# An attention and feed-forward block: a third staging buffer for the query and key products, the masking band in bf16, and weight preparation queued one microsecond behind its operands

## The chip, the core and the metric

The kernel runs on one core of one Trainium2 chip. The metric is the device time of one launch in microseconds. A core has five instruction queues that matter here: TensorE (PE, matrix products; its weight loads are shown as PEld), VectorE (DVE), ScalarE (ACT), GpSimdE (POOL) and SyncE (SP). SyncE only issues DMA transfers; ScalarE issues some as well, between its other instructions. Each queue runs in the order in which the program was written.

## The reference

One transformer block on 2048 rows of 640, with 32 heads of 20 and a window of 256 keys:

```
def _A_ref(x, wqkv, wo):
    qkv = (x @ wqkv).reshape(B, S, 3, H, Dh).transpose(2, 0, 3, 1, 4)
    q, k, v = qkv[0], qkv[1], qkv[2]
    scores = einsum("bhqd,bhkd->bhqk", q, k) * (Dh ** -0.5)
    mask = (idx[:, None] - idx[None, :] >= 0) & (idx[:, None] - idx[None, :] < W)
    scores = where(mask, scores, -1e9)
    o = einsum("bhqk,bhkd->bhqd", softmax(scores), v)
    return o.transpose(0, 2, 1, 3).reshape(B, S, D) @ wo

def _B_ref(x, w_gate, w_up, w_down):
    return (gelu(x @ w_gate) * (x @ w_up)) @ w_down

h  = x + _A_ref(layernorm(x), wqkv, wo)
h2 = h + _B_ref(layernorm(h), w_gate, w_up, w_down)     # F = 1536
```

Everything is float32.

## The kernel before

Float32 accuracy at half-precision speed comes from splitting. A matrix is written as a high half and a low half in float16 (names ending in `h` and `l`), and a product is made of three: high by high, low by high, high by low (`products`, L550). The first rows' value product is the exception: it runs on raw float32 weights held in `gu`, `h0h` and `h0l`. Where the planner finds room it runs a product as four products on quarters of the array side by side (`quarters`, L542).

The rows are cut in 16 blocks of 128 (`B[j]`) and 8 pairs of blocks (`c`). For each block the kernel loads the rows (`xt`), normalises them (`xp`), transposes the halves (`xh`, `xl`), and then a pair of blocks goes through the query and key products (`qk`, L736). `qk_out` (L761) evicts such a product from PSUM: ScalarE copies the high half into a staging tile `qks`, VectorE the low half, and ScalarE issues a DMA that writes both to a scratch tensor in DRAM, `qk<c><0 or 1>` (0 for queries, 1 for keys). `stack` (L783) reads it back with SyncE, six small copies for each stack, in the layout in which the score products need their operands (`qT`, `kT`). So `qk21` are the keys of pair 2, and the six copies `kT<-qk21` are one of its two stacks. The staging tile has two buffers, and `qk_out` starts only while fewer than two of the `qks` are unwritten: `pos["qk"]` counts those begun, `pos["qks"]` those whose write is issued.

For each block and each head, scores are computed twice. First come `maxima`: a product, on which `max_out` (L925) runs a VectorE operation that adds a mask and takes the row maximum. The mask is `band` (L614) for inner blocks: zero, with a large negative number above and below the allowed diagonals. Then comes the score product, transposed, with the maximum folded in as further rows; ScalarE takes the exponential into `pt`, GpSimdE clears what the window excludes, and TensorE multiplies by the values (`pv<-pt,v`). The result goes through the output projection `w3` into `h`, and the feed-forward part follows in three groups of 512 columns. Its last groups work on sums of halves (`ws`), made from the split weights after attention, when their buffers come free.

Weights are prepared beside attention. `load_slices` (L375) loads a 128-row slice (`wsl`) twice: once for VectorE to find the scale (`scale`, L389; its reduction reads the slice into `am`), and once for `split` (L435): ScalarE writes the high half (`gu<-wsl`), scales the slice in place (`wsl<-wsl`), and GpSimdE subtracts to get the low half. The output projection comes first (`wo`), then the first group's gate slices (from `in_wg_dram`) and up slices (from `in_wu_dram`).

What runs when is decided as the program is written, by a planner. `Clock` (L54) holds a modelled time for each engine, for each tile and for each DMA. Work is divided into lanes (generators), and a lane yields the engine that it wants and a function for the modelled time at which its operands are ready. The loop at the end steps a modelled time `now`; `Lane.start` (L1832) lets a lane queue its next instruction if its engine is free soon enough (`back`) and its operands are ready by `now + late`. `late` is 0.1 us, or minus `HELD` (1 us) for most of SyncE's transfers. So the instruction order on every queue is fixed by these numbers, and a small edit can move much. `split_lane` (L1679) and `scale_lane` (L1649) are the lanes of the weights. Until the first score is queued, the loop fills TensorE with products of the unit matrix (`pv<-ident16`, L1914) wherever nothing else is ready.

One property of the queues is seen in the instruction lists: SyncE's and ScalarE's DMAs take turns on eight landing semaphores. A DMA that gets a semaphore waits until the DMA that had it last has landed, also if that was issued by the other engine and has nothing to do with it.

All instructions are recorded by a helper, `Engine.call` (L199), so every row of the profile carries L199, and rows are told apart by the names of their tiles.

Of the kernel before, what the change touches and what calls it, by code (L numbers as in the profile page):

```python
# [11 lines left out]
F32 = mybir.dt.float32  # L12
F16 = mybir.dt.float16
BF16 = mybir.dt.bfloat16
# [8 lines left out]
P = 128  # L23
# [4 lines left out]
CW = 2 * P  # L28
# [21 lines left out]
def _pow2(e):  # L50
    return float(2.0 ** e)
# [202 lines left out]
def block_kernel(ctx: ExitStack, tc: tile.TileContext, x, wqkv, wo, wg, wu, wd, out):  # L254
    nc = Clock(tc.nc)
    const = ctx.enter_context(tc.tile_pool(name="const", bufs=1))
# [10 lines left out]
    opened, pos = Counter(), Counter()  # L267
# [14 lines left out]
    def done(name):  # L282
        opened[name] -= 1
# [23 lines left out]
    SWAY = 4  # L307
    BRIDGE = 0.2
    PATIENCE = 2.0

    def need(*reads, slots=(), when=None, eng="tensor"):

        def f():
            if when and not when() or any(opened[n] >= banks[n] for n in slots):
                return INF
            return max([nc.ready(reads, eng)]
                       + [nc.slot(psums[n], n, banks[n]) for n in slots])
        return f
# [4 lines left out]
    def on(eng, *reads, when=None, after=None):  # L323
        f = need(*reads, when=when, eng=eng)
        if after is not None:
            return (eng,), lambda: max(f(), nc.others(after, eng))
        return (eng,), f
# [14 lines left out]
    nc.vector.tensor_copy(ident16, ident)  # L342
    mhalf = const.tile([P, 1], F32, name="mhalf")
    nc.vector.memset(mhalf, -0.5)
    ones = const.tile([P, P], F32, name="ones")
    nc.vector.memset(ones, 1.0)


    NS = 16
# [110 lines left out]
    W = {}  # L460
# [89 lines left out]
    def products(n, term, ready=None, at_=None):  # L550


        ps = [at_[0]] if at_ else []
        col = at_[1] if at_ else 0

        def start(i):
            if ready and not ready(i) or not ps and opened["mm"] >= banks["mm"]:
                return INF
            t = nc.ready([x for ab in term(i) for x in ab], "tensor")
            return t if ps else max(t, nc.slot(psums["mm"], "mm", banks["mm"]))  # L560

        for i in range(n):
            yield ("tensor",), lambda i=i: start(i)
            if not ps:
                ps.append(bank("mm"))
            m = term(i)
            for k, (l, r) in enumerate(m):
                if k:
                    yield pe()
                o = ps[0][:, col:col + r.free_size()]  # L570
                quarters(o, l, r, start=(i == 0 and k == 0),
                         stop=(i == n - 1 and k == len(m) - 1))
                pos["dense"] += r.free_size() * 3 // len(m)
        return o
# [12 lines left out]
    def ff_scales_down(fg):  # L587
# [6 lines left out]
    wq = wqp.enter_context(tc.tile_pool(name="wq", bufs=1, side="right"))  # L594
    wp = attn.enter_context(tc.tile_pool(name="wp", bufs=1))
# [13 lines left out]
    HB = P // 2  # L609
# [1 line left out]
    nc.gpsimd.memset(mask, 0.0)  # L611
    nc.gpsimd.affine_select(mask[:, P:2 * P], mask[:, P:2 * P], pattern=[[-1, P]],
                            compare_op=ALU.is_ge, fill=NEG, base=0, channel_multiplier=1)
    band = wp.tile([P, 5 * HB], F32, name="band")  # L614
    nc.gpsimd.memset(band, 0.0)
    for a in range(2):
        first, last = band[HB * a:HB * a + HB, 0:HB], band[HB * a:HB * a + HB, 4 * HB:]
# [36 lines left out]
    qs = const.tile([P, 1], F32, name="qs")  # L654
# [81 lines left out]
    def qk(c, which):  # L736

        w = W["qk"[which]]
        first = c == which == 0
        if not first:  # L740
            xh, xl = C[c].x
            wh, wl = w.hl
        d = dram.tile([D, 2, CW], F16, name=f"qk{c}{which}")
        left = [3]
        for t0 in range(0, KC, 2):
            ts = range(t0, min(t0 + 2, KC))
            yield pe(slots=["mm"])
            ps = bank("mm")
            for i, t in enumerate(ts):
                fs = slice(t * P, (t + 1) * P)  # L750
                if first:
                    yield from products(KC, lambda k: [(w.raw[0, k][:, fs], x32[:, k, :])],
                                        at_=(ps, i * CW))
                    continue
                yield from products(KC, lambda k: parts((wh[:, k, fs], wl[:, k, fs]),
                                                        (xh[:, k, :], xl[:, k, :])),
                                    lambda k: k in w.have, (ps, i * CW))
            tasks.append(qk_out(c, which, ts, ps, d, left))
        C[c].used += 1

    def qk_out(c, which, ts, ps, d, left):  # L761

        o = ps[:, :len(ts) * CW].rearrange("p (t n) -> p t n", n=CW)
        up = qs if c == which == 0 else _pow2(QE)
        yield on("scalar", ps, when=lambda: pos["qk"] < pos["qks"] + 2 and (c or pos["qs"]))
        pos["qk"] += 1
        st = nc.tile(wq, [P, 2, 2, CW], F16, "qks", 2)
        hi, lo = (st[:, :len(ts), i, :] for i in range(2))
        nc.scalar.activation(hi, o, AF.Copy, scale=up)
        yield on("vector", hi, after=ps)  # L770
        nc.vector.scalar_tensor_tensor(lo, o, up, hi, op0=ALU.mult, op1=ALU.subtract)
        done("mm")
        both = st[:, :len(ts)].rearrange("p t m n -> p t (m n)")
        yield on("scalar", both)
        nc.scalar.dma_start(d[ts[0] * P:(ts[-1] + 1) * P].rearrange("(t p) m n -> p t (m n)", p=P),
                            both)
        pos["qks"] += 1
        left[0] -= 1
        if not left[0]:
            for blocks in [[2 * c, 2 * c + 1]] if c < 2 else [[2 * c], [2 * c + 1]]:  # L780
                side.append((LATE, stack(c, which, d, blocks)))

    def stack(c, which, d, blocks):  # L783
        last = blocks[-1]
        yield ("sync",), need(d, when=lambda: pos["big"] == 2 and (W["q"].ready if c < 2 else
                                                                B[last - 4].scored), eng="sync")
        if which == 0:
            for b in blocks:
                B[b].mx = at("mxs", [P, H], F32, 4)
        ring, n = ((qT, RQ), (kT, RK))[which]  # L790
        s = blocks[0] % n
        to = ring[:, :, s:s + len(blocks), :].rearrange("p i r n -> p i (r n)")
        cols = slice(blocks[0] % 2 * P, blocks[-1] % 2 * P + P)
        for par in range(2):
            for m, i in enumerate(((0, 0, 1), (0, 1, 0))[which]):
                rows = slice(64 * par + DH * m, 64 * par + DH * m + DH)
                if c > 1:
                    yield ("sync",), lambda: nc.moved["sync"] - PACE
                nc.sync.dma_start(to[rows], d.rearrange("(a d i) m n -> a m d i n", a=2,
                                                        d=DH)[par, i][:, :, cols])  # L800
        for b in blocks:
            B[b].stacked += 1
            if B[b].stacked == 2:
                for pr in range(0, H // 2, pairs(b)):
                    heapq.heappush(maxq, (b, pr))
# [327 lines left out]
    ffpools = [None, None]  # L1133
# [685 lines left out]
    class Lane:  # L1819
# [12 lines left out]
        def start(self, now):  # L1832

            if "tensor" in self.engs:
                if (self.gen.__name__ in ("normalise", "o_transpose") and nc.mode == "col"
                        and not B[-1].scored and self.need() <= nc.t["tensor"]):
                    self.since = min(self.since, nc.t["tensor"])
                    if nc.t["tensor"] < self.since + PATIENCE:
                        return False
                wait = BRIDGE if nc.kind == "col" and self is rows else 0.0  # L1840
                return (nc.t["tensor"] <= now + AHEAD
                        and self.need() <= max(now, nc.t["tensor"]) + wait)
            name = self.gen.__name__
            back = self.back
            if name in ("split_lane", "scale_lane"):
                back = PREP if not W["o", 0].ready else FFPREP
            elif name == "x_lane":
                back = EARLY if not B[XF].full else LATE
            elif name == "max_out" and not W["v"].ready:
                back = RAMPMAX  # L1850
            if isinstance(self.engs, Soon):
                back = max(back, OUT)
            if ffpools[1]:
                back = FFBACK.get(name, OUT)
            late = 0.1 if self.engs != ("sync",) or name in ("stack", "load_lane") else -HELD
            return (all(nc.t[e] <= now + back for e in self.engs if e != "sync")
                    and self.need() <= now + late)

# [109 lines left out]
```

## Time and profile before

| | |
|---|---|
| time, median of 3 runs | 1001.67 us (1001.38 to 1004.41) |
| the profiled execution: time, span | 1003.55 us, 1001.8 us |
| TensorE products, weight loads | 15101 each |
| VectorE, ScalarE, GpSimdE instructions | 2246, 859, 498 |
| DMA traffic | 112.97 MB, 113 GB/s on average |
| first score maximum on TensorE | 53.20 us |
| last exponentials and values of attention | about 562 us |
| lowest granted clock of the 40 slices | 0.8, in the slice from 150 us |

A page of the profile gives each engine's busy time and its share of the span, then the span in 40 slices with the busy tenths and the clock that TensorE was granted, then the chain of work that ended last, followed back from the last instruction. The trace behind the page is asked for stretches, timelines of an engine, single tiles and waits. In a row `out<-in` names the tile written and those read, with partitions and elements; `x4` means that many such instructions; the bracket gives the idle time of the engine ahead of the row and what ended it. Products are pipelined, so their lengths overlap, and what one costs is the distance of two starts.

### The profile page before, as it was taken

Reading aid. Unit: us, or ns where it says so; the run is one execution under the profiler, and the core shown is the slowest. Engines: PE = TensorE matmul, PEld = TensorE weight load, DVE = VectorE, ACT = ScalarE, POOL = GpSimd, SP = SyncE. Lnnn points to the kernel's source line nnn. Section 1 sums busy time; section 2 is a strip of 40 time slices with the busy share of each in tenths; the row PEclk is TensorE's granted clock in tenths of the full one; section 3 lists DMA queues with packets and bytes.
Section 4 is the critical chain, followed back from the end, with each engine's and each line's share of the span. In section 5 each row is a group of like instructions: output and inputs, shape, how many; then the busy total and the mean of one; then the engine's idle time right before and its main releaser. Section 6 shows DMA issues by size and latency. Waiting matters only on the chain.

```text
span 1001.8 us, 35343 instructions
## 1 busy us (share of the span) xinstructions
PE 979.5 (98%) x15101; PEld 747.0 (75%) x15101; DVE 788.6 (79%) x2246; ACT 486.4 (49%) x859; POOL 340.9 (34%) x498
## 2 busy tenths in 40 slices
PE   8998997999999999999999999999999999999998
PEld 8875775777787777777656754588788888888886
DVE  7878997887877876676688697897986877788784
ACT  5516564855555655555577634343223333443431
POOL 7003344544433433333345301253403222232320
PEclk9999998999999999999999999999999999999999
DMA  8657755652433523123315342234453442223211
GB/s 312 130 129 170 174 144 162 161 131 64 106 94 71 116 77 95 50 75 83 122 30 140 61 143 81 82 130 133 132 185 100 144 152 79 79 75 112 80 54 53
DMA packets 129613, 112.97 MB, mean 113 GB/s; under 512 B 85168, under 2 KB 103344, under 8 KB 129456
## 3 DMA queue, kind: packets, MB, share of 16 engines
q1 hardware_dynamic: 117360, 99.97, 35.6%
q10 hardware_dynamic: 12096, 10.75, 3.5%
q8 instruction: 118, 1.93, 0.8%
q14 instruction: 39, 0.32, 0.1%
HBM read 73.73 MB, written 28.84 MB: 102 GB/s over the span
## 4 chain that ended last, share of the span: by engine, by line
PE 77%; DVE 6%; DMA 2%; ACT 2%; issue 1%; POOL 1%; SPq 0%; ACTq 0%; DVEq 0%; POOLq 0%
PE mm L199 35%; PE rb L199 12%; PE ra L199 11%; PE pv L199 10%; PE tp L199 9%; DVE ts L199 1%; DVE am L199 1%; DVE gel L199 1%; DMA wst<-in_wu_dram 1%; DVE al L199 1%; DVE ws L199 0%; DVE ht L199 0%; DVE junk L199 0%; DMA wsl<-in_wg_dram 0%; DMA qk<-qks 0%
## 5 line engine op out<-in xcount | busy, mean ns | idle before, releaser
L199 POOL TENSOR_SCALAR_AFFINE_SELECT pt<-pt 128x512 f32<-128x512 f32 x352 | 174.8, 512 | 272.6 <-ACT pt L199 254.5
L199 DVE CUSTOM_DVE_ANT_0 junk<-ra,band 128x320 bf16<-128x320 f32 x230 | 112.5, 489 | 42.8 <-PE ra L199 37.7
L199 ACT ACTIVATE pt<-rb,esc 128x640 f32<-128x640 f32 (+2 forms) x131 | 99.7, 768 | 92.9 <-PE rb L199 77.2
L199 DVE CUSTOM_DVE_ANT_0 junk<-rb,band 128x320 bf16<-128x320 f32 x218 | 106.6, 489 | 34.6 <-PE rb L199 29.6
L199 ACT ACTIVATE pt<-ra,esc 128x640 f32<-128x640 f32 (+2 forms) x125 | 95.0, 767 | 73.1 <-PE ra L199 61.5
L199 PE MATMUL pv<-pt,v 128*21 128x128 f32 x2880 | 103.5, 276 | 0.8 <-ACT oT L199 0.6
L199 PEld LDWEIGHTS <-ah 128*128 128x128 f16 x648 | 63.4, 98 | 23.5 <-issue 1.2
L199 PEld LDWEIGHTS <-ws 128*128 128x128 f16 x720 | 70.4, 98 | 13.0 <-issue 3.0
L199 PEld LDWEIGHTS <-qT 60*64 60x64 f16 x1280 | 29.8, 104 | 65.7 <-issue 55.4
L199 PEld LDWEIGHTS pv<-pt,v 128*21 128x21 f32 x2880 | 69.3, 101 | 10.5 <-issue 1.0
L199 PEld LDWEIGHTS <-kT 62*64 62x64 f16 x2880 | 64.7, 107 | 10.3 <-issue 6.9
L199 PEld LDWEIGHTS <-gu 128*128 128x128 f16 (+1 forms) x709 | 51.9, 98 | 25.7
L199 DVE SCALAR_TENSOR_TENSOR ht<-mm,ffk,ht 128x320 f32<-128x320 f32 x86 | 46.9, 545 | 16.4 <-PE mm L199 15.2
L199 PE MATMUL mm<-xh,w1h 128*32 128x256 f16 (+1 forms) x356 | 56.6, 276 | 1.4 <-DVE qks L199 1.4
L199 PE MATMUL mm<-xl,w1h 128*32 128x256 f16 (+1 forms) x368 | 56.5, 276 | 0.0
L199 PE MATMUL mm<-xh,w1l 128*32 128x256 f16 (+1 forms) x362 | 56.5, 274 | 0.0
L199 ACT CAST ah<-gel 128x512 f16<-128x512 f32 x48 | 29.6, 617 | 53.3 <-DVE gel L199 51.8
L199 DVE TENSOR_TENSOR al<-gel,ah 128x512 f16<-128x512 f32 x48 | 42.9, 893 | 14.9 <-ACT ah L199 14.2
L199 ACT ACTIVATE gel<-gel,ffk 128x512 f32<-128x512 f32 x36 | 26.0, 722 | 54.5 <-DVE gel L199 54.4
L199 PE MATMUL mm<-w3h,ol 128*32 128x320 f16 (+1 forms) x322 | 49.6, 301 | 0.0
L199 PE MATMUL mm<-w3l,oh 128*32 128x320 f16 (+1 forms) x319 | 49.4, 301 | 0.0
L199 PE MATMUL mm<-w3h,oh 128*32 128x320 f16 (+1 forms) x310 | 49.4, 299 | 0.0
(354 smaller groups left out, 2670.0 us busy)
## 6 DMA issues: line engine op xcount, KB each, us to landing
ws<-wsums SPq DMA_DIRECT2D x24, 640.0 KB
qk<-qks ACTq DMA_DIRECT2D x32, 256.0 KB
wsums<-ws SPq DMA_DIRECT2D x12, 640.0 KB
qT<-qk SPq DMA_DIRECT2D x72, 80.0 KB
kT<-qk SPq DMA_DIRECT2D x72, 80.0 KB
ht<-in_x_dram SPq DMA_DIRECT2D x16, 320.0 KB
h_dram<-ht SPq DMA_DIRECT2D x16, 320.0 KB
ht<-h_dram SPq DMA_DIRECT2D x16, 320.0 KB
```

The source lines that it names most:

```text
L199: r = real(*args, **kw)
```

## The change

Four edits:

- The staging tile `qks` gets three buffers instead of two, and `qk_out` may start while fewer than three are unwritten. That takes 2048 bytes more of each partition.
- `band` is kept in bf16 instead of float32 (640 bytes a partition less). Its values are 0 and -1e30.
- `ones`, a float32 tile of 128 by 128 that nothing reads, is left out (512 bytes less).
- In `Lane.start`, once the output projection is ready and until the feed-forward buffers are open, work of `split_lane` and `scale_lane` is queued only if its operands have been ready for one modelled microsecond (`SETTLE`).

```diff
@@ -307,6 +307,7 @@
     BRIDGE = 0.2
     PATIENCE = 2.0
+    SETTLE = 1.0
@@ -342,8 +343,6 @@
-    ones = const.tile([P, P], F32, name="ones")
-    nc.vector.memset(ones, 1.0)
@@ -611,7 +610,7 @@
-    band = wp.tile([P, 5 * HB], F32, name="band")
+    band = wp.tile([P, 5 * HB], BF16, name="band")
@@ -762,9 +761,9 @@
-        yield on("scalar", ps, when=lambda: pos["qk"] < pos["qks"] + 2 and (c or pos["qs"]))
+        yield on("scalar", ps, when=lambda: pos["qk"] < pos["qks"] + 3 and (c or pos["qs"]))
         pos["qk"] += 1
-        st = nc.tile(wq, [P, 2, 2, CW], F16, "qks", 2)
+        st = nc.tile(wq, [P, 2, 2, CW], F16, "qks", 3)
@@ -1853,6 +1852,8 @@
             late = 0.1 if self.engs != ("sync",) or name in ("stack", "load_lane") else -HELD
+            if name in ("split_lane", "scale_lane") and W["o", 0].ready and not ffpools[0]:
+                late = -SETTLE
             return (all(nc.t[e] <= now + back for e in self.engs if e != "sync")
                     and self.need() <= now + late)
```

Since the planner's order follows from these numbers, the instructions move. TensorE has 14046 matrix instructions in the program instead of 13603; all of the difference comes from products that run as four quarters (829 instead of 651), and fillers are 144 instead of 235. The order of the last 2813 products is unchanged. Three places:

**TensorE before the first maxima.** Before, the raw value product (`mm<-gu`, `mm<-h0h,gu`, `mm<-h0l,gu`) alternates with small transposes, and where it stops waiting for room, the fillers begin (`pv<-ident`; a run of 86 of them follows).

```order
L199 MATMUL mm<-gu 128x320
L199 MATMUL ra<-ident,am_386 128x128
L199 MATMUL mm<-h0h,gu 128x320
L199 MATMUL rb<-ident,pt 128x128 x4
L199 MATMUL tp<-ident,pt 128x128
L199 MATMUL mm<-h0h,gu 128x320
L199 MATMUL mm<-h0l,gu 128x320 x2
L199 LDWEIGHTS ident_81
L199 MATMUL pv<-ident_81 128x128
```

Now, on the same queue and at the same place:

```order
L199 MATMUL mm<-gu 128x320
L199 MATMUL mm<-h0h,gu 128x320
L199 MATMUL tp<-ident,pt 128x128
L199 MATMUL mm<-h0h,gu 128x320
L199 MATMUL mm<-h0l,gu 128x320
L199 MATMUL rb<-ident,pt 128x128
L199 MATMUL mm<-h0l,gu 128x320
L199 MATMUL mm<-gu 128x320
L199 MATMUL mm<-h0h,gu 128x320 x2
L199 MATMUL mm<-h0l,gu 128x320 x2
L199 LDWEIGHTS w0h
```

The fillers at this place are gone, and the query products (`w0h`) follow at once. The value product of the second block pair moves behind the first maxima, and 184 products of 256 columns stand ahead of the first maximum instead of 97.

**SyncE around the last gate slices.** Before, the two last gate slices (`wsl<-in_wg_dram`) stand among the copies of the key stacks of pair 2 (`kT<-qk21`):

```order
L199 DMA xt_2815<-in_x_dram 128x640
L199 DMA kT_126<-qk21_2287 20x16x128 x2
L199 DMA ht_2949<-in_x_dram 128x640
L199 DMA kT_126<-qk21_2287 20x16x128 x5
L199 DMA wsl_3044<-in_wg_dram 128x512
L199 DMA kT_126<-qk21_2287 20x16x128
L199 DMA wsl_3088<-in_wg_dram 128x512
```

Now these stacks are through before, and the first up slices (`wsl<-in_wu_dram`) stand among the stacks of pair 3 (`qT<-qk30`, `kT<-qk31`):

```order
L199 DMA_TRANSPOSE xl_2951<-xp_3027 128x5x128
L199 DMA xt_3371<-in_x_dram 128x640
L199 DMA wsl_3673<-in_wg_dram 128x512
L199 DMA wsl_3716<-in_wg_dram 128x512
L199 DMA qT_125<-qk30_2568 20x16x128 x2
L199 DMA wsl_3770<-in_wu_dram 128x512
...
L199 DMA kT_124<-qk31_3164 20x16x128
L199 DMA wsl_3940<-in_wu_dram 128x512
L199 DMA kT_124<-qk31_3164 20x16x128 x3
L199 DMA wsl_4005<-in_wu_dram 128x512
L199 DMA wsl_4007<-in_wu_dram 128x512
```

The two gate slices moved out of the key stacks, and four up slices (numbers 3770, 3940, 4005 and 4007 here) moved in among the stacks of the next pair.

**ScalarE at the last gate splits.** Before, the split of a slice (`gu<-wsl`, `wsl<-wsl`) stands between the exponentials (`pt`) that follow the 40th, and the write of `qk30` (`DMA qk30<-qks`) directly ahead:

```order
L199 DMA qk30_2653<-qks_3048 128x512
L199 ACTIVATE pt_3100<-ra_3101,esc_130 128x2x320
L199 ACTIVATE gu_99<-wsl_2605,sw_88 128x512
L199 ACTIVATE wsl_2605<-wsl_2605,sw_88 128x512
L199 ACTIVATE pt_3100<-rb_3155,esc_130 128x2x320
L199 ACTIVATE gu_99<-wsl_3044,sw_88 128x512
L199 ACTIVATE wsl_3044<-wsl_3044,sw_88 128x512
```

Now, with the exponentials that follow the 48th:

```order
L199 ACTIVATE pt_3793<-ra_3794,esc_128 128x2x320
L199 DMA qk40_3644<-qks_3783 128x2x512
L199 ACTIVATE gu_97<-wsl_3673,sw_86 128x512
L199 ACTIVATE wsl_3673<-wsl_3673,sw_86 128x512
L199 ACTIVATE gu_97<-wsl_3716,sw_86 128x512
L199 ACTIVATE pt_3793<-rb_3844,esc_128 128x2x320
L199 ACTIVATE wsl_3716<-wsl_3716,sw_86 128x512
```

The splits moved eight exponentials further down, behind the first write of `qk40`; the splits of the up slices moved from the 54th to 59th exponential to the 69th to 74th.

## The prediction

> **What bounds the kernel now.** I read the page first: busy time of each engine, the granted clock, and the chain that ended last.
>
> ```profile
> PE 979.5 (98%) x15101; PEld 747.0 (75%) x15101; DVE 788.6 (79%) x2246; ACT 486.4 (49%) x859; POOL 340.9 (34%) x498
> PEclk9999998999999999999999999999999999999999
> PE 77%; DVE 6%; DMA 2%; ACT 2%; issue 1%; POOL 1%; SPq 0%; ACTq 0%; DVEq 0%; POOLq 0%
> PE mm L199 35%; PE rb L199 12%; PE ra L199 11%; PE pv L199 10%; PE tp L199 9%; DVE ts L199 1%; DVE am L199 1%; DVE gel L199 1%; DMA wst<-in_wu_dram 1%; DVE al L199 1%; DVE ws L199 0%; DVE ht L199 0%; DVE junk L199 0%; DMA wsl<-in_wg_dram 0%; DMA qk<-qks 0%
> ```
>
> TensorE is busy for 98% of the span and makes 77% of the chain. The change leaves its useful products as they are, so it can only win the time in which TensorE waits, runs fillers or has a lower clock. The clock row has one 8, in the slice from 150 to 175 us. The next view is therefore the table of busy time by stretches (span, then PE, PEld, DVE, ACT, POOL, granted clock, DMA share, GB/s).
>
> ```profile
> 24.00:76.00 52.00, 50.59 (x533) 40.23 (x533) 41.73 (x158) 19.68 (x40) 1.65 (x3) 1.00 0.63 128
> 92.00:100.00 8.00, 5.56 (x79) 3.25 (x81) 7.15 (x23) 5.34 (x9) 3.99 (x4) 0.83 0.72 201
> 158.00:163.20 5.20, 0.62 (x24) 0.38 (x13) 0.57 (x4) 2.20 (x4) 0.70 (x2) 0.89 0.69 171
> 163.20:170.00 6.80, 6.80 (x93) 4.54 (x93) 5.03 (x15) 2.36 (x5) 3.56 (x6) 0.58 0.62 193
> 200.00:450.00 250.00, 249.89 (x6263) 193.88 (x6255) 188.71 (x701) 142.00 (x220) 99.35 (x206) 1.00 0.35 88
> ```
>
> From 200 to 450 us TensorE loses 0.11 us of 250: nothing is to be had there. The holes are before. The largest is at 158 us, and the timelines of TensorE and of ScalarE say what it is (start, length, operation, and in brackets the idle time before it and what ended it).
>
> ```profile
> 158.11 0.35 PE L199 MATMUL mm<-w3h,ol 128*32 128x320 f16 x4
> 158.25 0.35 PE L199 MATMUL mm<-w3h,oh 128*32 128x320 f16 x4
> 163.18 0.48 PE L199 MATMUL ra<-kT,qT 60*64 60x320 f16 x4 [4.58 <-ACT pt L199]
> ```
>
> ```profile
> 155.24 0.77 ACT L199 ACTIVATE pt<-rb,esc 128x640 f32<-128x640 f32 x1
> 160.91 0.72 ACT L199 ACTIVATE gu<-wsl,sw 128x512 f16<-128x512 f32 x1 [4.90 <-DMA wsl<-in_wg_dram]
> 162.35 0.78 ACT L199 ACTIVATE pt<-ra,esc 128x640 f32<-128x640 f32 x1
> ```
>
> TensorE waits 4.58 us for a score exponential (`pt<-ra`), and that stands in ScalarE's queue behind a weight split (`gu<-wsl`) whose slice has not landed. Why the slice is late stands in SyncE's timeline, its waits between 130 and 200 us, and the chain of waits from 142 to 165 us.
>
> ```profile
> 148.81 7.64 SPq L199 DMA_DIRECT2D kT<-qk  x5
> 156.55 0.46 SPq L199 DMA_DIRECT2D wsl<-in_wg_dram  x1
> ```
>
> ```profile
> SPq L199 <- DMA qk<-qks: 13.1, 5, 3.8
> ```
>
> ```profile
> 142.98 3.65 DMA qk<-qks
> ...
> 156.55 4.33 DMA wsl<-in_wg_dram
> ```
>
> Five stack copies took 7.64 us of SyncE's queue. One copy alone takes about 0.75, so half of it is a wait, 3.8 us at the longest, for the landing of a `qk` write which ScalarE issued. SyncE's and ScalarE's transfers share a ring of landing semaphores, so a stack copy can wait for a write that it doesn't read. The slice is issued at 156.55 and lands 4.33 us later.
>
> **The change, part by part.** Sums are against the profiled execution, 1003.55 us (span 1001.8 and 1.75 around it). It lies 1.88 above the median 1001.67 of the runs shown, and I subtract that at the end.
>
> *The stall at 158 us.* In the new order the two late gate slices stand behind no stack copies on SyncE, and their splits come 8 exponentials later on ScalarE (48 to 51 instead of 40 to 45) while only splits that have been ready for 1 us are queued. The wait of 4.58 us goes, and with it the slow clock behind it: 6.80 us at 0.58 lost 6.80 x (1 - 0.58) = 2.86. Together **-7.4**. What is late next is one term further down. The other end is 0, if the stall only moves.
>
> The row says that a hole of 4.58 us brings 6.8 us near half clock. [...]
>
> *The start.* Ahead of the first maxima the old order issued 86 fillers (`pv<-ident`) in one piece, and the new order has 144 fillers instead of 235 in the kernel.
>
> ```profile
> 37.66 4.96 PE L199 MATMUL pv<-ident 128*128 128x128 f16 x86
> 42.46 0.76 PE L199 MATMUL mm<-gu 128*128 128x320 f32 x2
> ...
> 53.20 0.31 PE L199 MATMUL ra<-kT,qT 60*64 60x128 f16 x8
> ```
>
> The piece lasts 42.46 - 37.66 = 4.80, so a filler costs 56 ns and 91 of them 5.1 us. In the new order the copies of the third buffer are made early and dense products stand where the fillers stood. Against it: on SyncE the last copy of the first key stack now waits, through the shared ring, for `qk` write 10, which ScalarE issues where TensorE is at product 294, and the first maximum is product 355. The 61 products between are 61 x 52.00/533 = 6.0 us. What must happen is the landing of the write (3.65), one issue (0.74, next row: the six copies of one stack took 40.66 to 47.44 with waits, the rows above 1.57 for two) and a landing of the copy, for which I take 3.65 again: 8.0. So the maxima come 2.0 late.
>
> ```profile
> 40.66 6.78 SPq L199 DMA_DIRECT2D kT<-qk  x6
> 146.65 1.57 SPq L199 DMA_DIRECT2D kT<-qk  x2
> ```
>
> The term is -5.1 + 2.0 = **-3.1**. Its ends are -5.1 (the write lands early) and +0.5: the time from the end of the six copies to the first maximum was 53.20 - 47.44 = 5.8 and may have been needed in full (3.65 + 0.74 + 5.8 - 6.0 = 4.2 late), with the clock of the 92 to 100 row behind it, 8.00 x 0.17 = 1.4.
>
> *The new wait.* The five late "up" slices now stand on SyncE among the 12 stack copies of `qk30` and `qk31`. One of them, the fourth (wsl_4007), waits through the ring for the second write of `qk40`, which ScalarE issues 50 products later. Its reader on VectorE (the reduction that finds the slice's largest value) stands 143 products behind the issue, so 93 behind that write: 93 x 250.00/6263 = 3.7 us. The slice needs the landing of the write, the issue and its own landing, 3.65 + 0.46 + 4.33 = 8.4: it is 4.7 us late for its reader. Behind the reader VectorE has maxima and the low halves of `qks`, ahead of the exponentials. If the stop passes on as the old one did (4.58 of 4.90) with the same clock, it costs 7.4 x 4.7/4.90 = 7.1. If VectorE's idle time (250.00 - 188.71 = 61 of 250 us) takes it up, it costs nothing. No row is nearer to one end, so I take the middle, **+3.5**, ends 0 and 7.1.
>
> *The weights after attention.* Between the last output projection and the first use of the summed weights `ws`, the new order leaves 24 products of 320 columns fewer, since they were done earlier. The chain that makes these weights starts when attention ends, and it is as long as before.
>
> ```profile
> 156.74 0.31 PE L199 MATMUL mm<-w3h,ol 128*128 128x320 f16 x1
> ...
> 157.16 0.30 PE L199 MATMUL mm<-w3h,ol 128*128 128x320 f16 x1
> ```
>
> ```profile
> 649.29 0.30 PE L199 MATMUL mm<-w10h,ah 128*128 128x320 f16 x1 [1.03 <-DVE ht L199]
> ```
>
> ```profile
> L199 PEld LDWEIGHTS <-ws x720: 95/98/98, 655.2 to 980.4; 128*128 128x128 f16 x180
> ...
> L199 DVE SCALAR_TENSOR_TENSOR ws<-ws,w9h x4: 807/818/2025, 653.2 to 674.8; 128x640 f16<-128x640 f16 x4
> ```
>
> One such product is (157.16 - 156.74)/3 = 0.14 us, so the cover is 3.4 us shorter. The first `ws` leaves VectorE at 653.2 + 0.82 = 654.0 and is read at 655.2, which is 1.2 us of room; already TensorE waited 1.03 us at 649.29. I take 3.4 - 1.2 = **+2.2**, ends 0 (other products fill it) and 3.4.
>
> *Changes of array mode.* The new order has 521 changes between whole and split array, 7 fewer.
>
> ```profile
> 170.86 0.27 PE L199 MATMUL mm<-xh,w1l 128*128 128x256 f16 x1
> 170.97 0.27 PE L199 MATMUL mm<-xh,w1h 128*128 128x256 f16 x1
> 171.17 0.33 PE L199 MATMUL ra<-kT,qT 60*64 60x320 f16 x4
> ```
>
> Products follow each other by 0.11; at the change it is 0.20. Seven times 0.09 is **-0.6** (the other end is 0). More products run as four quarters (829 instead of 651); four quarters side by side take the time of one whole product (the `x4` rows at 158.11 and 158.25 lie 0.14 apart, as the `x1` rows above), so this is 0.
>
> *The band in bf16, and `ones` gone.*
>
> ```profile
> L199 DVE CUSTOM_DVE_ANT_0 junk<-ra,band x230: 468/491/493, 94.6 to 530.1; 128x320 bf16<-128x320 f32 x115
> L199 DVE MEMSET ones<- x1: 165/165/165, 1.7 to 1.7; 128x128 f32 x1
> ```
>
> The masking maximum takes 491 ns, 230 times here and 218 on the other bank. No row shows it with a two-byte band. If it took half, VectorE would win 448 x 0.245 = 110 us; if it took a tenth longer it would lose 22, against the 61 idle of 250 us above. Neither is on the path (the chain gives `DVE junk` 0%), so the time changes by **0**; ends 0 and +2.2, if a tenth of those 22 us reached TensorE. The set of `ones` is 0.165 us of VectorE before anything waits for it: 0.
>
> **Sum**: -7.4 - 3.1 + 3.5 + 2.2 - 0.6 = -5.4, so 1003.55 - 5.4 = 998.15, and against the median 996.3.
>
> **The rivals.**
> 1. *The up slices are covered.* VectorE's idle time and what TensorE has queued take up the late reduction. For it: the VectorE share. Against it: a late slice stopped ScalarE, which was idle half of the time, and the stop came through. Then 996.3 - 3.5 = 992.8.
> 2. *The stop moves and doubles; this one ends slower than before.* A second up slice (wsl_3940) waits in the same way for the first write of `qk40`. If both stop VectorE, and TensorE pays 7.1 for each, 3.5 becomes 14.2 and the time 1007.0. It decides from 3.5 + 5.4 = 8.9 us of new waits on: above this the change loses. For it: the ring wait of 3.8 us is in the trace. Against it: the earlier write lies closer, and a mean VectorE gap of a quarter stands against it.
> 3. *The change doesn't do what it says.* The gate slices move with their stack copies in time, the split still waits, and a hole with its clock stays: +7.4, so 1003.7. Against it: the two slices stand two places behind a load, and the five entries ahead of them are no stack copies.
> 4. *Both give-backs are hidden.* The first maxima wait for nothing and other products fill the weights' chain: 996.3 - 2.0 - 2.2 = 992.1.
>
> **How the numbers follow.** Chances: my forecast 0.38, rival 1 0.22, rival 4 0.15, rival 2 0.13, rival 3 0.12. A measurement of this kernel tells about 0.3% (3.0 us) from no change, so faster means under 998.7 and slower over 1004.7. Rivals 1 and 4 are faster. The forecast lies 2.4 inside the bound and three quarters of it count as faster, the rest as no difference: 0.285 + 0.22 + 0.15 = 0.65 faster. Rival 3 and that rest give 0.22, rival 2 0.13. The lower end takes all gains without a give-back: 1001.67 - 5.1 - 7.4 - 0.6 = 988.6, rounded to 989. The upper end stands at 1004, just behind rival 3; rival 2 and the tail of low bounds are left out.
>
> **What would show it.** The gap of 4.58 us before `ra<-kT,qT` is gone, ScalarE has no wait of over 2 us for `wsl<-in_wg_dram`, and the clock row has no 8 from 150 to 175 us. The tile of fillers has 144 rows. A wait of VectorE for `wsl<-in_wu_dram`, with a TensorE hole behind it, would show the new wait, and its absence rival 1. In the stretch from 600 to 663 us TensorE would lose about 2 us more than before. The forecast fails if a hole of several us opens ahead of the first maxima, or if the stretch from 200 to 450 us, which lost 0.11 us, loses more than one: then a term that I set at nothing is at work.

## The result

The changed kernel takes 1008.82 us (median of 7 runs, 1005.66 to 1012.24), the kernel before 1001.67 (7 runs, 999.13 to 1004.41). The ratio is 1.0073, with a 95% interval from 1.0052 to 1.0093: slower by 0.7%, where 996.3 was forecast, and outside the range of 989 to 1004.

The page of the changed kernel, busy time, clock and chain:

```profile
span 1007.1 us, 36216 instructions
PE 976.3 (97%) x15544; PEld 745.0 (74%) x15544; DVE 793.1 (79%) x2245; ACT 486.6 (48%) x859; POOL 338.3 (34%) x498
PEclk9999999999999999999999999999999999999999
PE 74%; DVE 14%; DMA 5%; ACT 3%; issue 2%; POOL 1%; SPq 1%; ACTq 0%; DVEq 0%
```

The 8 in the clock row is gone, but TensorE's share of the chain fell from 77% to 74% and VectorE's rose from 6% to 14%. The table of stretches says where. First the stretches that the prediction showed, then two behind attention (span, PE, PEld, DVE, ACT, POOL, granted clock, DMA share, GB/s):

```profile
24.00:76.00 52.00, 50.02 (x545) 38.96 (x543) 42.61 (x161) 20.63 (x42) 1.97 (x3) 1.00 0.64 148
92.00:100.00 8.00, 8.00 (x153) 6.37 (x152) 7.50 (x29) 3.50 (x8) 1.00 (x2) 1.00 0.24 61
158.00:163.20 5.20, 5.20 (x163) 4.51 (x155) 4.52 (x24) 3.58 (x5) 3.01 (x7) 1.00 0.76 133
163.20:170.00 6.80, 5.84 (x122) 4.43 (x111) 5.91 (x20) 6.14 (x10) 5.37 (x8) 1.00 0.57 166
200.00:450.00 250.00, 249.77 (x6469) 195.08 (x6462) 189.72 (x697) 146.15 (x228) 105.29 (x211) 1.00 0.38 93
...
645.00:680.00 35.00, 29.55 (x228) 23.30 (x226) 28.70 (x45) 11.71 (x23) 16.77 (x12) 0.90 0.27 100
680.00:725.00 45.00, 41.72 (x340) 33.87 (x338) 40.27 (x66) 14.45 (x31) 18.03 (x12) 0.96 0.50 142
```

The same two stretches behind attention in the kernel before:

```profile
645.00:680.00 35.00, 33.30 (x278) 27.06 (x277) 32.07 (x55) 13.16 (x26) 18.75 (x14) 1.00 0.30 113
680.00:725.00 45.00, 42.80 (x364) 35.35 (x363) 39.22 (x68) 14.94 (x33) 19.65 (x12) 1.00 0.44 133
```

Up to 170 us the stall is gone as forecast: no hole at 158 us, and full clock. The hole at 93 us, for which the forecast had no term, is gone too. Most of the loss is behind attention, at 645 to 725 us, where TensorE is 4.8 us less busy and at a lower clock, though from 663 us on its products stand in the order of before. TensorE's timeline of the changed kernel there, rows with a wait and two that follow:

```profile
651.06 1.25 PE L199 MATMUL tp<-ts,ws 128*128 128x256 f16 x5 [3.36 <-DVE ws L199]
652.10 1.27 PE L199 MATMUL ra<-ts,ws 128*128 128x256 f16 x5
...
663.49 0.70 PE L199 MATMUL tp<-ts,ws 128*128 128x256 f16 x5 [0.63 <-DVE am L199]
677.60 0.71 PE L199 MATMUL ra<-h0h,w6l 128*128 128x256 f16 x5 [0.87 <-DVE rs L199]
683.17 0.71 PE L199 MATMUL ra<-h0h,w9h 128*128 128x256 f16 x5 [0.51 <-ACT rs L199]
717.17 0.70 PE L199 MATMUL tp<-h1l,ws 128*128 128x256 f16 x5 [2.77 <-ACT rr L199]
```

TensorE reaches the summed weights `ws` early, waits 3.36 us for them, then runs at half clock (five products in 1.04 us instead of 0.55), and meets one wait after another. Behind the last of them it runs at half clock once more. The granted clock of the two slow pieces:

```profile
651.00:657.05 6.05, 5.99 (x26) 3.82 (x27) 1.99 (x4) 0.74 (x2) 2.74 (x2) 0.50 0.72 286
718.40:721.90 3.50, 3.50 (x20) 2.49 (x18) 3.50 (x5) 1.42 (x3) 0.97 (x1) 0.52 0.61 160
```

To compare kernels with different orders I cut each trace at four places and count what TensorE loses: the distance of each two products, less the price of the first by the rows of before (0.109, 0.136 and 0.216 us for 256, 320 and 512 columns, a quarter of it in a quad, 0.1 for a change of mode). In us:

| profiled execution | before | changed |
|---|---|---|
| a sixth of the value products done at | 193.1 | 185.8 |
| five sixths done at | 494.3 | 487.2 |
| last value product at | 561.5 | 559.9 |
| last output projection at | 575.5 | 573.0 |
| dense products left from there to the first late weight `w6` | 73.2 | 69.9 |
| from the last output projection to the last product, less those | 349.0 | 360.1 |
| last product at | 997.7 | 1003.1 |

The 7 us won by 186 us still stand at 487. At the end of attention 1.6 are left of them, and the part behind it takes 11.1 longer than its products.

The first line of the table scatters between executions. Three other profiles in which TensorE has the order of before up to 566 us or further (the band alone, `ones` counted, and before with the first down projection held, all below) reach that place at 190.9, 190.0 and 189.6 us. Three others with the order of the changed kernel up to 535 us or further reach it at 187.8, 187.0 and 187.6. By these eight profiles the lead is about 4 us, not 7.3. Behind that place there is little scatter: from there to the last product before takes 804.6 us (804.1 and 804.2 in the first two of the other profiles), the changed kernel 817.3 and 816.4.

### The profile page after: what moved, and what is told of

Its sections match the earlier page's. It is cut to its first block, busy times and chain, and to the rows that moved or that the text cites. A ratio compares the mean times of both kernels' runs of the same rounds, so it can differ in the third digit from the quotient of the medians.

```text
span 1007.1 us, 36216 instructions
## 1 busy us (share of the span) xinstructions
PE 976.3 (97%) x15544; PEld 745.0 (74%) x15544; DVE 793.1 (79%) x2245; ACT 486.6 (48%) x859; POOL 338.3 (34%) x498
## 4 chain that ended last, share of the span: by engine, by line
PE 74%; DVE 14%; DMA 5%; ACT 3%; issue 2%; POOL 1%; SPq 1%; ACTq 0%; DVEq 0%
PE mm L199 35%; PE rb L199 11%; PE ra L199 11%; PE pv L199 10%; PE tp L199 8%; DVE junk L199 2%; DVE ws L199 1%; DVE gel L199 1%; DVE wsl L199 1%; DVE ht L199 1%; ACT pt L199 1%; DMA wsl<-h_dram 1%; POOL pt L199 1%; DVE al L199 1%; DVE am L199 1%
## 5 line engine op out<-in xcount | busy, mean ns | idle before, releaser
L199 PEld LDWEIGHTS <-ah 128*128 128x128 f16 (+1 forms) x669 | 64.0, 98 | 22.9 <-issue 0.3
```

The lines of the kernel that those rows point to most:

```text
L199: r = real(*args, **kw)
```

## The experiments

**The edits one at a time.** Theory A: the time depends on where the order puts weight slices and dense products. Theory B: only the buffer and the delay matter.

The band alone:

```diff
-    band = wp.tile([P, 5 * HB], F32, name="band")
+    band = wp.tile([P, 5 * HB], BF16, name="band")
```

> Before with the band alone in bf16; every queue has the instructions of before in the same order. Theory (the band is free): the masking maximum stays at 0.49 us, within 0.3% of before. Rival (its width is part of the loss): maxima longer by 0.02 us or more, time over 1004.

1001.69 us, ratio 0.9998 (0.9979 to 1.0018). The maximum with a bf16 band, in this run's trace:

```profile
L199 DVE CUSTOM_DVE_ANT_0 junk<-ra,band x230: 468/492/494, 95.9 to 528.0; 128x320 bf16<-128x320 f32 x115
```

The median is 492 ns where before had 491: the width of the mask costs and wins nothing here.

Without `ones` alone:

```diff
-    ones = const.tile([P, P], F32, name="ones")
-    nc.vector.memset(ones, 1.0)
```

> Before without the unused tile of ones alone. It is 0.165 us of VectorE that nobody waits for, but the planner counts it, and without it every queue comes out in another order (262 fillers instead of 235). Theory A (the time depends on where the order happens to put weight slices and dense products): moves by 2 us or more in either direction, with other holes than before. Theory B (only the buffer and the delay matter): within 1.5 us of before.

1013.41 us, ratio 1.0119 (1.0079 to 1.0159). Taking away 0.165 us that nobody waits for costs 12 us. ScalarE's timeline shows the old hole at a new place, with a second wait for the same kind of slice:

```profile
171.07 0.72 ACT L199 ACTIVATE gu<-wsl,sw 128x512 f16<-128x512 f32 x1 [4.80 <-DMA wsl<-in_wg_dram]
...
174.50 0.79 ACT L199 ACTIVATE pt<-rb,esc 128x640 f32<-128x640 f32 x1 [1.75 <-DMA wsl<-in_wg_dram]
```

Theory A holds, and the size is a warning: an edit that the planner notices can move this kernel by a per cent.

The delay alone:

```diff
+            if name in ("split_lane", "scale_lane") and W["o", 0].ready and not ffpools[0]:
+                late = -SETTLE
```

> Before with the delay of weight work alone (two buffers, band and ones as before; 235 fillers; the order up to the first gate splits is that of before). Theory A (the hole at 158 us goes, and dense products that are used earlier come back as holes at the end of attention and after it): 996 to 1001, the hole at 158 us gone. Rival (the delay makes the weights late, and it is the source of the loss): 1004 to 1009, with waits for weights behind it.

1002.28 us, ratio 1.0003 (0.9984 to 1.0023). The time lies between the ranges of theory A and of the rival, and the profile is theory A's: no wait of over 0.7 us from 150 to 180 us, a sixth of the values done at 188.9 (before 193.1). But the last sixth of attention takes 72.3 us instead of 67.1, so the last values come at 562.2.

The buffer, with the band and without `ones`, but without the delay:

```diff
-        yield on("scalar", ps, when=lambda: pos["qk"] < pos["qks"] + 2 and (c or pos["qs"]))
+        yield on("scalar", ps, when=lambda: pos["qk"] < pos["qks"] + 3 and (c or pos["qs"]))
...
-        st = nc.tile(wq, [P, 2, 2, CW], F16, "qks", 2)
+        st = nc.tile(wq, [P, 2, 2, CW], F16, "qks", 3)
```

> The changed kernel without the delay: third buffer, band in bf16, no ones (144 fillers, 3.3 us more products than before between the output projection and the first use of the late weights). Theory A: fillers give 5.1 us, nothing is given back there: 993 to 999. Rival (the third buffer is the source of the loss): 1005 to 1010.

997.43 us, ratio 0.9955 (0.9937 to 0.9974): faster, inside theory A's range. So neither the buffer nor the delay loses by itself; together, in the order that the planner then wrote, they do.

**The products left behind attention.** A rule holds the first down projection back (`HOLD` is 1), in the changed kernel and, in the second run, in before:

```diff
+                if pos["early"] >= HOLD:
+                    yield pe(when=lambda: woq and W["o", 0].ready or all(b.wrote for b in B))
+                    continue
...
                 tasks.append(down_out(c, fg, b, nh, ps))
+                pos["early"] += 1
```

> The changed kernel with one rule more: of the first down projection only 12 products may come ahead of the end of the output projection (the changed kernel has 60 there, the version with the buffer alone 12). The order is that of the changed kernel up to that place, 6.6 us of products move behind it. Theory A (too few products are left beside the weight chain after attention, which is serial): the waits for the summed weights (3.5 us at 647, and those to 720) go, 998 to 1003. Rival (the delay itself makes the later weights late, or the tail is slow for another reason): 1006 to 1010.

1009.3 us, ratio 1.008 (1.0049 to 1.0111). Theory A as stated missed. The products moved, and the tail got shorter (353.6 us instead of 360.1, by the last line but one of the table), but TensorE's timeline has new holes where they had been:

```profile
564.93 0.63 PE L199 MATMUL tp<-ident,o 128*128 128x128 f32 x4 [1.76 <-DVE o L199]
566.96 0.48 PE L199 MATMUL tp<-ident,o 128*128 128x128 f32 x1 [1.40 <-DVE ol L199]
```

The last block's own steps run one behind the other there, and the products that were moved had covered them: the last output projection still ended at 573.8 (changed 573.0).

> Before with the rule of the first experiment of this group: 12 products of the first down projection ahead of the end of the output projection instead of 36, 3.3 us more behind it. Theory A: before lost about 2 us at 638 to 660 to the chain; it wins 1 to 3 us, 998.5 to 1001. Rival: no change, 1001 to 1002.5.

1003.98 us, ratio 1.0018 (0.9998 to 1.0039): no win, and above both ranges. A wait of 1.3 us for `ol` opens at the same place.

Two other lengths of the delay give other orders:

```diff
-    SETTLE = 1.0
+    SETTLE = 1.25
```

> The changed kernel with a delay of 1.25 us instead of 1.0. The order that comes out has 76.5 us of dense products between the last output projection and the first late weight, as with the buffer alone (changed kernel: 69.9). Theory A: the time follows the products left, 995 to 1000. Rival (the longer the delay, the later the weights): at or over the changed kernel, 1008 to 1012.

1002.2 us, ratio 1.001 (0.9991 to 1.0029): between the two. With a longer delay it is some 6 us better than the changed kernel, which goes against the rival, but worse than theory A said.

> The changed kernel with a delay of 0.75 us; the order has 69.9 us of products after the last output projection, as the changed kernel. Theory A: 1004 to 1010, with a wait of about 3 us for the summed weights near 647. Rival (a shorter delay costs less): 999 to 1004.

1010.13 us, ratio 1.0088 (1.0054 to 1.0121): with as few products left as in the changed kernel, as slow as it, and the loss ahead of the first `ws` is 3.5 us again. The half clock behind that wait is missing in this profile, though (last section), and the tail is 4 us shorter than the changed kernel's.

**When attention ends.** The theory was amended: the weight chain behind attention is serial, and feed-forward products ahead of the last scores push back its start and are missing beside it. The rule is now on the first gate and up products (`GATES` is 7, in the last of these runs 6):

```diff
+                if pos["gates"] >= GATES and not B[-1].scored:
+                    yield pe(when=lambda: woq and W["o", 0].ready or B[-1].scored)
+                    continue
```

> The changed kernel with one rule: of the 8 product groups of the first gate and up projection only 7 may come before the last block's scores are done (the changed kernel does all 8 there and begins the down projection; the version with the buffer alone does 7). Order as in the changed kernel up to that place; 4.3 us of feed-forward products move from before the last scores to behind them. Theory A, amended (what counts is when attention ends, since the weight chain behind it is serial; feed-forward products ahead of the last scores push that end back, and products held later than that don't help, as the rule on the down projection showed): last values at about 556 instead of 560, time 997 to 1003. Rival (the chain is late for another reason): the last values come earlier, but the time stays at 1006 to 1010.

1005.03 us, ratio 1.0032 (1.0016 to 1.0048). In the same group the changed kernel was run again:

> The changed kernel once more, for a second profile: the waits for the summed weights (3.5 us near 647) and for the normalised rows (2.9 us at 714) should stand at the same places if the order makes them, 1006 to 1010. If they were chance, they move.

1009.85 us, ratio 1.0083 (1.0062 to 1.0104). TensorE's busy time in the stretches behind attention, and its first wait there, are those of the first profile to the hundredth:

```profile
645.00:680.00 35.00, 29.55 (x226) 23.13 (x224) 29.41 (x45) 12.23 (x24) 16.70 (x12) 0.90 0.25 95
...
652.20 1.25 PE L199 MATMUL tp<-ts,ws 128*128 128x256 f16 x5 [3.36 <-DVE ws L199]
```

So those holes are made by the order, not by chance. (Their place is 1.1 us later, as the start was slower.) With the rule (the order is the same up to its place) the stretch is nearly that of before, and the wait for `ws` is gone:

```profile
645.00:680.00 35.00, 33.16 (x276) 26.77 (x274) 32.24 (x57) 11.85 (x25) 17.71 (x12) 1.00 0.30 113
```

That takes 4.8 us from the changed kernel's time, by medians of one chip, and leaves it 2 us above the theory's range. The half of the amended theory on the tail holds. The other half missed: the last values came at 562.3, not at 556. Small waits opened in the last sixth, most of them for VectorE (TensorE is idle for 3.3 us there instead of 1.3 to 1.5), and the start was 1.8 us slower than in the first profile.

> Before with the same rule (before does all 8 groups ahead of the last scores): 3.2 us of products move behind them. Theory A, amended: last values 3 us earlier, time 998 to 1001. Rival: 1001 to 1004.

1005.6 us, ratio 1.0044 (1.0023 to 1.0064): worse than either range. Before had enough products left, and taking some from the last scores opens holes there (2.3 us idle in the last sixth instead of 0.5).

> The buffer without the delay, with 6 groups instead of 7 ahead of the last scores. Theory A, amended: last values 3 us earlier than with the buffer alone; if the last block leaves no new hole, 994 to 997, and at best the fastest version. Rival (the last block's own waits open, as they did with the rule on the down projection): 997 to 1001.

1002.69 us, ratio 0.9999 (0.998 to 1.0017): the rival's case, and 1.7 us above its range: TensorE is idle for 3.8 us in the last sixth instead of 0.2.

**Combination or order.** The last group leaves the edits and changes the order only. Where the set of `ones` stood, the planner is told its time. First in before, with the band in bf16, then in the changed kernel, then with the buffer alone; the last run is the changed kernel with `SETTLE = 0.25`, without this line:

```diff
+    nc.t["vector"] += 0.065 + 0.00106 * P
```

> Before without the tile of ones and with the band in bf16, but the planner still counts the 0.2 us of the set, so that every queue has the instructions of before in the same order, the set left out. Theory (the removal acts only through the order): within 0.3% of before, 999 to 1004. Rival (the removal itself shifts the start): 1008 to 1014, as without ones alone.

1002.56 us, ratio 1.0023 (1.001 to 1.0036). TensorE has the order of before, product for product, and the removal costs 0.1 to 0.4%, 11 us less than without the count. The 12 us came through the order.

> All edits of the change, but the planner still counts the set of ones. Another order comes out: 140 fillers, 76.5 us of products after the last output projection (changed kernel 69.9), 85.0 after the last values (80.9). Theory A, amended: the holes after attention are missing, 994 to 1002. Rival (buffer and delay don't go together): 1006 to 1011.

996.22 us, ratio 0.9962 (0.9944 to 0.998). All four edits, and it is faster than before by 0.4%, where the changed kernel is slower by 0.7%. The stretches behind attention:

```profile
645.00:680.00 35.00, 33.96 (x292) 28.35 (x290) 28.84 (x50) 14.11 (x30) 15.93 (x10) 1.00 0.19 77
680.00:725.00 45.00, 42.80 (x365) 35.46 (x363) 40.96 (x82) 13.85 (x31) 17.47 (x10) 1.00 0.59 152
```

> The buffer without the delay, with the planner still counting the set of ones: 140 fillers, 71.6 us of products after the last output projection, 80.5 after the last values, so as few as in the changed kernel. Theory A, amended: holes after attention as in the changed kernel, 1002 to 1009. Rival (without the delay there is no loss): 995 to 1000, as with the buffer alone.

1003.81 us, ratio 1.0028 (1.001 to 1.0045): the buffer without the delay now loses, in an order with 71.6 us of products left.

> The changed kernel with a delay of 0.25 us: 76.5 us of products after the last output projection, 84.9 after the last values. Theory A, amended: 995 to 1001. Rival: 1004 to 1010.

1003.48 us, ratio 1.0025 (1.0006 to 1.0044). A miss: the tail is free of the extra holes, as expected, but the last sixth takes 70.9 us.

All profiled executions side by side, with the last sixth of attention (from five sixths of the value products to the last) and the tail (the last line but one of the table above):

| kernel | time, median | last sixth | products left | tail less products |
|---|---|---|---|---|
| before | 1001.67 | 67.1 | 73.2 | 349.0 |
| delay alone | 1002.28 | 72.3 | 74.8 | 348.8 |
| buffer, band, no `ones` | 997.43 | 67.3 | 76.5 | 350.1 |
| all edits, `ones` counted | 996.22 | 67.5 | 76.5 | 348.3 |
| buffer, `ones` counted | 1003.81 | 72.9 | 71.6 | 353.1 |
| delay 0.75 | 1010.13 | 73.2 | 69.9 | 355.9 |
| changed | 1008.82 | 72.8 | 69.9 | 360.1 |
| changed, again | 1009.85 | 72.5 | 69.9 | 359.7 |
| changed, down projection held | 1009.3 | 72.8 | 76.5 | 353.6 |
| changed, gate products held | 1005.03 | 71.6 | 76.5 | 349.8 |
| delay 1.25 | 1002.2 | 67.3 | 76.5 | 352.5 |
| delay 0.25 | 1003.48 | 70.9 | 76.5 | 349.3 |
| band alone | 1001.69 | 67.1 | 73.2 | 348.2 |
| no `ones` alone | 1013.41 | 64.3 | 74.8 | 349.0 |
| before, `ones` counted | 1002.56 | 67.1 | 73.2 | 348.7 |
| before, down projection held | 1003.98 | 67.1 | 76.5 | 349.9 |
| before, gate products held | 1005.6 | 67.6 | 78.1 | 350.1 |
| buffer, gate products held | 1002.69 | 68.3 | 81.6 | 349.7 |

Orders with 73 us or more left have tails of 348 to 350, with two exceptions (353.6 and 352.5); orders with fewer have 353 to 360. The orders fall into two kinds in the last sixth, 64 to 68 and 71 to 73 us, and each kind has orders with the delay and orders without.

The traces say what the longer kind does there. By the prices of before it holds 67 to 69.5 us of dense products, the shorter kind 61 to 65; the exception is the changed kernel with gate products held, which has 64.5 and the waits told above. The changed kernel has 4.5 us more of them than before: 2.7 of the output projection, 1.3 of the first down projection and 0.5 of transposes.

The two exceptions in the tail have waits of their own. With the delay of 1.25 TensorE waits 3.19 us at 710 us, where before waits 2.20, and then runs at half clock for 5.9 us. With the down projection held it waits 0.87 us for the first `ws` and 2.78 us at 719, and runs at half clock for 3.4 us behind that.

## Why the prediction was wrong

Measured terms compare the two first profiles, in idle time of TensorE by its rows or in losses by the prices above.

- **The stall at 158 us**, -7.4: right in kind, and its size was partly luck. From 158 to 170 us TensorE's idle time fell from 4.58 to 0.96 us, and the 2.86 us of slow clock are gone: -6.5. The delay alone removes the hole too. But the size of the stall is that of one execution. The same stretch in before, and in three kernels with the same TensorE order up to there (the band alone, before with the down projection held, before with `ones` counted):

```profile
158.00:170.00 12.00, 7.42 (x113) 4.93 (x102) 5.60 (x19) 4.56 (x8) 4.26 (x7) 0.72 0.65 183
158.00:170.00 12.00, 8.56 (x196) 6.66 (x192) 8.76 (x31) 5.86 (x9) 5.10 (x8) 1.00 0.83 210
158.00:170.00 12.00, 10.05 (x211) 7.42 (x206) 8.26 (x31) 6.69 (x10) 5.67 (x10) 0.86 0.76 206
158.00:170.00 12.00, 9.24 (x186) 6.72 (x176) 7.35 (x28) 6.51 (x10) 4.75 (x8) 0.86 0.77 196
```

  The idle time is 4.58, 3.44, 1.95 and 2.76 us, and the granted clock 0.72 to 1.00. The hole at 93 us (2.44 us idle) went as well, and new waits of 1.2, 0.8 and 1.0 us opened at 88, 112 and 167 us; the sum had a term for neither.
- **The start**, -3.1: right in kind. 91 fillers fewer are 5.1 us; losses up to and with the first row of maxima rose by 1.1. The first maximum came 0.5 us earlier, and a wait for `kT` of 0.75 us stands in the first row of maxima, where the late copy was expected. Measured -4.0. (The issue of 0.74 us in that sum is 0.79 by its row, 1.57 for two.)
- **The new wait**, +3.5: right, and smaller. VectorE's waits from 180 to 192 us and TensorE's holes behind them are in the changed kernel's trace:

```profile
DVE am L199 <- DMA wsl<-in_wu_dram: 3.2, 4, 1.4
```

```profile
188.09 0.34 PE L199 MATMUL rb<-qT,kT 62*64 62x128 f16 x12 [0.79 <-DVE mxs L199]
191.16 0.34 PE L199 MATMUL ra<-qT,kT 62*64 62x128 f16 x12 [1.11 <-DVE mxs L199]
```

  Four up slices were late, not one, by 1.4 us at most: about 2.2 us of TensorE, with no lower clock.
- **Changes of array mode**, -0.6: no run isolates it, and it is too small to be told from the rest.
- **Band and `ones`**, 0: right for the band and for the set itself. But each alone was not what was built: `ones` matters through the order.
- **The weights after attention**, +2.2 with ends 0 and 3.4: **this step failed.** The mechanism was right, the size was not. It measured 11.1. The first wait came as described: TensorE stood ready for the first `ws` 7.7 us earlier than before (651.06 less a loss of 3.5, against 655.2), and got it 4.2 us earlier. The sum took this wait for the whole price. It left out the slow clock behind the wait, which it had charged behind the stall at 158 us, and took the chain to be level with TensorE afterwards. From the first `ws` to 725 us the losses rose from 3.4 to 10.7: 2.9 us at half clock behind the first wait, 1.8 at half clock behind the wait at 717, and 2.5 of further waits, for weights and for steps that stand behind weight work on VectorE and ScalarE. Another 2.2 came near 790. Against that, 1.9 us that before lost ahead of its first `ws` are gone.
- **What I left out**: the end of attention. 4.5 us more of dense products and about 1.1 more of holes lie in its last sixth, so that 7.1 us of lead became 1.6. I priced what the new order does at the first places where it differs and took the rest to be level. From 450 us to the last sixth, TensorE's idle time rose from 0.6 to 2.2 us too.

None of the rivals named this. The one on the slow side put the loss on the up slices, which cost 2.2 us. The forecast's own test, that 600 to 663 us would lose some 2 us more, pointed at the right stretch (its idle time rose by 2.2 us), but it had no clock and stopped too early.

What is shown: the four edits are not slow together (996.22 us in another order); the removal of `ones` acts through the order; the first waits behind attention come again at the same places, and go when products are left for them (4.8 us); the last sixth is longer where more products stand in it. What stays open: why the planner's rules put more products there in some orders than in others, and what sets the scatter of 2 to 3 us ahead of 193 us.

## What to carry to other kernels

Where a planner writes the order, an edit's own cost says little: compare the whole order, above all how much independent work is left beside each serial chain, and run the edits in a second order before judging them. A microsecond won early is only worth what the last serial stretch leaves of it; work that fills a hole early is missing as cover later. A wait at the head of a chain isn't its whole price if the links behind it stay late, or if the clock falls, as behind the first `ws` (2.9 us). Price a stall from several executions: the one at 158 us was 2.0 to 4.6 us long.

## What the runs showed of the hardware

The same hole does not always bring the lower clock. TensorE's timelines of before and of the version with the buffer alone, at the same products:

```profile
715.62 0.71 PE L199 MATMUL tp<-h1l,ws 128*128 128x256 f16 x5 [2.20 <-ACT rr L199]
716.17 0.71 PE L199 MATMUL tp<-h1h,w5h 128*128 128x256 f16 x5
716.71 0.71 PE L199 MATMUL ra<-h1h,w5l 128*128 128x256 f16 x5
```

```profile
708.39 0.71 PE L199 MATMUL tp<-h1l,ws 128*128 128x256 f16 x5 [2.20 <-ACT rr L199]
708.94 1.06 PE L199 MATMUL tp<-h1h,w5h 128*128 128x256 f16 x5
709.80 1.27 PE L199 MATMUL ra<-h1h,w5l 128*128 128x256 f16 x5
```

Both wait 2.20 us. Before goes on at full speed, five products in 0.55 us; the other falls to half speed 0.8 us later and stays there for about 3.4 us, which costs 1.6. Over the 18 profiles of this case, the wait at this place was 2.20 us twelve times, and half speed followed in two of them; it was 2.77 us five times, and half speed followed each time, for 3.2 to 3.4 us. After a wait of 3.36 us for the first `ws` both profiles of the changed kernel ran at half speed for 5.9 us. With the delay of 0.75 the same wait was followed by full speed:

```profile
653.44 0.72 PE L199 MATMUL tp<-ts,ws 128*128 128x256 f16 x5 [3.37 <-DVE ws L199]
654.18 0.72 PE L199 MATMUL ra<-ts,ws 128*128 128x256 f16 x5
```

So in these profiles the price of such a hole was its length and, in some executions, up to 2.9 us more (5.9 us at half speed).

How far the landing semaphores are shared is in the trace of before: its 502 transfers, 422 issued by SyncE and 80 by ScalarE, name eight of them, and each of the 494 transfers that use one again was issued after the earlier transfer on it had landed. Ten of SyncE's loads before 17 us waited for the landing of a load of `qT` or `gu`, 5.3 us in all and 0.8 us at the longest. The stack copy ahead of the late slice at 158 us waited in the same way: a `qk` write that ScalarE issued at 151.68 us landed at 155.69, and SyncE issued the copy, on the same semaphore, at 155.70. In the changed kernel, too, 502 transfers name eight semaphores.
